# One source order for VectorE, ScalarE and GpSimd in attention, with decoding and the memory term cut into one phase per step

## The chip, the cores and the metric

The kernel runs on one core of one Trainium2 chip. The time is the device time of one execution in microseconds (us); the kernel before was timed three times, and the median of the three is its time. One further execution was profiled, and all rows below are from that one.

## What is computed

Inputs are fp32: q, k, v of shape (4, 8, 576, 64), a memory `M_prev` per head, and six weight matrices.

```python
scores = q @ k.T / 8, causal;  a = softmax(scores);  local = a @ v
q_p = phi(q)                                   # max(q, 0) + exp(min(q, 0))
mem = (q_p @ M_prev) / (q_p @ z_prev + 1e-6)
x = g * mem + (1 - g) * local                  # g = sigmoid(beta), per head
x = x.transpose(0, 2, 1, 3).reshape(2304, 512)
x = ((x @ w1) * (x @ w2)) @ w3 @ w_out         # 512 -> 1024 -> 1024 -> 512
h = x @ w_in                                   # 512 -> 2048
out = (h - tanh(h)) @ w_out2                   # 2048 -> 512
```

## The kernel before

**Weights.** The weights lie in memory as 64-bit patterns. A tile of 128 x 512 of them is loaded (`dec_load`, L64, tile `raw`) and decoded on the chip by `dec_ops`: GpSimd clamps the high words into T (L72) and makes E from them (L75), ScalarE rescales T (L77) and writes the low words into E (L79), VectorE merges the two (L82). The fp32 value is then split into two parts that are multiplied apart: GpSimd copies the high part (L94), VectorE subtracts it for the low part (L97). A `Decoder` runs this in four phases per tile. Where an fp32 product is wanted with such weights, three matmuls are issued: high x high, high x low, low x high.

**Folding.** `w3 @ w_out` is multiplied out beforehand, as 16 folds (f = 0..7 in two halves), during attention: 28 tiles are decoded there (8 of w_out, 16 of w3, 4 of w1 and w2), and `fold_pe` issues the matmuls in pieces: three matmuls a piece, four pieces a fold, 64 pieces in all (tile `fo`). After a fold ScalarE evacuates the first half (L268), or VectorE adds the second to it (L271) and the sum is split (L273, L274).

**Attention.** There are 16 pairs of heads P. Each has four steps, m = 4P + s: at s = 0 the row blocks u = 0 and 1 (128 rows each), at s = 1, 2, 3 the blocks u = 2, 3, 4 (the last has 64 rows). A step computes `scores` on TensorE (PSUM tile `sc`, 2 buffers), `rmax` (VectorE's reduction for the row maxima, L362), `exps` (ScalarE, L374, with the row sums), and `norm` (VectorE's reciprocal of the sums, L382 and L383, then GpSimd scales p by it, L388). Two steps later (`WAIT` = 2) `trans` transposes p on TensorE (PSUM tile `t`, 2 buffers), and `copy` moves it to SBUF as g0, g1 or g2: ScalarE four times in five (L399), VectorE else (L401). `av` multiplies g by v for the pair before: group 0 at s = 0, group 1 at s = 2; these are the matmuls `o<-g,v`, x20 for group 1. The pieces of the folds stand in the steps as `PIECES` says: 1, 2, 0 and 2 for the first eight pairs, 1, 1, 0 and 2 after. q and k of a pair are one tile `r` (3 buffers): SyncE issues its load (`load_qk`, L189) at s = 0, two pairs ahead, and ScalarE scales q by 1/8 (`scale_q`, L196) at s = 1 of the pair before its use.

**Memory term.** The first of six groups of 384 tokens is done within attention (`mem_early`), the other five later. For three tiles of 128 tokens (tile `mw`) `mem_a` runs on VectorE, ScalarE and GpSimd (products at L511 and L519), `mem_b` transposes (tile `mt`), and `mem_mm` does eight matmuls for each half of the heads (tile `mo`) and adds the result to x (L542). Tile `o` in PSUM has two buffers, which av, folds and `mo` share.

**What sets the order.** Only TensorE is held to the order of the source (`pinned`, L147). On VectorE, ScalarE, GpSimd and SyncE the scheduler picks by its own estimate of when an instruction can start. The background (decoding and the memory term) is given to it by `pump`, 2.2 times a step (`PACE`; 3.2 for the first `LEAD` = 10), each a phase, not before the step's maxima and exponentials (`issue_after`, `mark`). After attention (some 273 us) come the stages of the weight products, which the diff doesn't touch.

## Time and profile before

| what | us |
|---|---|
| three runs | 1012.65, 1011.66, 1015.96 |
| median | 1012.65 |
| profiled execution, its own time | 1016.29 |
| its span | 1014.5 |
| its mean granted clock (1 is full) | 0.988 |
| busy: TensorE | 959.7 (95%) |
| busy: weight loads | 818.1 (81%) |
| busy: VectorE | 660.1 (65%) |
| busy: ScalarE | 633.6 (62%) |
| busy: GpSimd | 409.1 (40%) |

The shares are means over all stages. The span runs from the first instruction to the last, and 1.8 us lie around it. PE is TensorE's matmuls, PEld its weight loads, DVE VectorE, ACT ScalarE, POOL GpSimd, SP SyncE. A number in square brackets behind an instruction is the time for which its engine stood idle before it, with what ended that time.

### The profile page before, as it was taken

Reading aid. Unit: us, or ns where it says so; the run is one execution under the profiler, and the core shown is the slowest. Engines: PE = TensorE matmul, PEld = TensorE weight load, DVE = VectorE, ACT = ScalarE, POOL = GpSimd, SP = SyncE. Lnnn points to the kernel's source line nnn. Section 1 sums busy time; section 2 is a strip of 40 time slices with the busy share of each in tenths; the row PEclk is TensorE's granted clock in tenths of the full one; section 3 lists DMA queues with packets and bytes.
Section 4 is the critical chain, followed back from the end, with each engine's and each line's share of the span. In section 5 each row is a group of like instructions: output and inputs, shape, how many; then the busy total and the mean of one; then the engine's idle time right before and its main releaser. Section 6 shows DMA issues by size and latency. Waiting matters only on the chain.

```text
span 1014.5 us, 16205 instructions
## 1 busy us (share of the span) xinstructions
PE 959.7 (95%) x5912; PEld 818.1 (81%) x5912; DVE 660.1 (65%) x1153; ACT 633.6 (62%) x1428; POOL 409.1 (40%) x500
## 2 busy tenths in 40 slices
PE   5899998969999899999999999999999999999998
PEld 2466555535698789999999999999999999998996
DVE  3655556766478765443212478888787787878875
ACT  5777767766655554244222668777776676767765
POOL 5757666765367552232000875222222222222222
PEclk9799999999999999999999999999999999999999
DMA  6443453433045562133000110000000000000000
GB/s 233 137 135 118 139 177 110 136 110 109 2 139 178 162 182 90 40 91 117 1 1 1 42 42 1 1 22 11 1 32 1 1 32 1 32 1 1 32 1 31
DMA packets 25807, 68.28 MB, mean 67 GB/s; under 512 B 4864, under 2 KB 5632, under 8 KB 25728
## 3 DMA queue, kind: packets, MB, share of 16 engines
q1 hardware_dynamic: 25728, 67.26, 20.8%
q8 instruction: 46, 0.75, 0.3%
q14 instruction: 33, 0.27, 0.1%
HBM read 62.53 MB, written 4.72 MB: 66 GB/s over the span
## 4 chain that ended last, share of the span: by engine, by line
PE 72%; DVE 8%; ACT 8%; DMA 6%; POOL 3%; issue 2%; SPq 0%; DVEq 0%; POOLq 0%; ACTq 0%
PE o L153 22%; PE h L153 20%; PE ab L153 15%; PE x L153 7%; DMA mw<-in_qt 3%; ACT p L374 3%; DMA r<-in_qk 2%; PE sc L153 2%; PE t L156 2%; PE fo L153 2%; DVE st L362 1%; ACT E L79 1%; POOL p L388 1%; ACT g L399 1%; ACT T L77 1%
## 5 line engine op out<-in xcount | busy, mean ns | idle before, releaser
L897 POOL TENSOR_TENSOR gl<-s,gh 128x384 fp32r<-128x384 f32 x96 | 99.6, 1038 | 287.9 <-ACT gh L891 273.0
L388 POOL TENSOR_SCALAR p<-p,st 128x128 f32<-128x128 f32 (+2 forms) x144 | 91.0, 645 | 59.5 <-ACT T L77 33.1
L153 PE MATMUL ab<-xh,wa 128*128 128x384 f32 x384 | 107.3, 340 | 4.3 <-DVE xs L542 3.2
L153 PE MATMUL x<-abh,wf 128*128 128x384 f32 x384 | 105.7, 340 | 2.2 <-ACT abh L696 2.2
L374 ACT ACTIVATE p<-sc,st 128x128 f32<-128x128 f32 (+2 forms) x144 | 78.0, 555 | 45.9 <-DVE st L362 39.3
L153 PE MATMUL ab<-xh,wb 128*128 128x384 f32 x384 | 105.7, 336 | 0.0
L873 DVE SCALAR_TENSOR_TENSOR s<-s,u 128x384 f32<-128x384 f32 x96 | 84.0, 875 | 25.0 <-ACT s L863 24.1
L869 ACT ACTIVATE u<-u,pc 128x384 f32<-128x384 f32 x96 | 59.4, 619 | 46.5 <-DVE s L873 46.5
L693 DVE TENSOR_TENSOR a<-ab,a 128x384 f32<-128x384 f32 x48 | 26.6, 553 | 83.2 <-PE ab L153 81.8
L153 PE MATMUL sc<-r 64*64 64x128 f32 (+4 forms) x640 | 72.2, 486 | 8.4 <-ACT r L196 5.9
L156 PE MATMUL t<-ident,p 128*128 128x128 f32 (+1 forms) x400 | 59.4, 285 | 21.6 <-ACT g L399 15.4
L75 POOL TENSOR_SCALAR E<-raw 128x512 f32<-128x512 f32 x72 | 59.5, 827 | 41.6 <-DVE z2p L82 7.6
L153 PEld LDWEIGHTS ab<-xh,wa 128*128 128x128 f32 x384 | 70.2, 188 | 7.2 <-DVE xs L542 4.8
L156 PEld LDWEIGHTS t<-ident,p 128*128 128x128 f32 (+1 forms) x400 | 46.2, 143 | 36.1 <-POOL p L388 16.8
L153 PEld LDWEIGHTS x<-abh,wf 128*128 128x128 f32 x384 | 70.1, 188 | 3.4 <-ACT abh L696 2.9
L861 ACT ACTIVATE u<-h 128x384 f32<-128x384 f32 x96 | 46.7, 487 | 41.5 <-PE h L153 41.5
L879 DVE TENSOR_TENSOR t<-h,t 128x384 f32<-128x384 f32 x96 | 53.1, 553 | 29.6 <-ACT t L862 29.2
L362 DVE TENSOR_REDUCE st<-sc 128x2 f32<-128x256 f32 (+4 forms) x80 | 62.5, 798 | 14.3 <-PE sc L153 13.4
L153 PEld LDWEIGHTS ab<-xh,wb 128*128 128x128 f32 x384 | 70.1, 188 | 0.3 <-ACT a L692 0.3
L878 DVE SCALAR_TENSOR_TENSOR s<-s,s 128x384 f32<-128x384 f32 x96 | 63.4, 661 | 8.7 <-DVE s L873 0.5
L72 POOL TENSOR_SCALAR T<-raw 128x512 f32<-128x512 f32 x72 | 52.3, 726 | 37.8 <-DMA raw<-in_wo 8.7
L79 ACT ACTIVATE E<-raw 128x512 uint16<-128x512 uint32 x72 | 56.8, 789 | 15.7 <-POOL E L75 14.9
(211 smaller groups left out, 2574.7 us busy)
## 6 DMA issues: line engine op xcount, KB each, us to landing
raw<-in_wo SPq DMA_DIRECT2D x24, 512.0 KB, 3.5
r<-in_qk SPq DMA_DIRECT2D x15, 576.0 KB, 4.6
raw<-in_w3t SPq DMA_DIRECT2D x16, 512.0 KB, 3.5
raw<-in_w SPq DMA_DIRECT2D x16, 512.0 KB, 3.5
raw<-in_wi SPq DMA_DIRECT2D x16, 512.0 KB, 3.5
v<-in_vt SPq DMA_DIRECT2D x16, 320.0 KB, 3.0
mw<-in_qt SPq DMA_DIRECT2D x18, 256.0 KB, 3.5
out<-ob SPq DMA_DIRECT2D x18, 256.0 KB, 2.3
```

The lines of the kernel that those rows point to most:

```text
L75: PO.tensor_scalar(out=e[:].bitcast(F32), in0=hw, scalar1=2.0 ** -100, scalar2=2.0 ** -53, op0=ALU.mult, op1=ALU.mult)
L79: AC.activation(out=e16, in_=lw, func=AF.Copy, scale=LOW_SCALE, bias=LOW_BIAS)
L153: return pinned(PE.matmul(o, lhsT, rhs, start=start, stop=stop))
L156: return pinned(PE.transpose(o, i, ident))
L362: mark["V"][m] = DV.tensor_reduce(out=st[:, 2 * x:2 * x + w], in_=seen(m, u, a), axis=AX.X if u < 4 else AX.XY, op=ALU.max, negate=True).ins
L374: mark["A"][m] = AC.activation(out=p[:, h], in_=sc[:, h], func=AF.Exp, bias=st[:, y:y + 1], accum_out=st[:, 4 + y:5 + y]).ins
L388: PO.tensor_scalar(out=pr, in0=pr, scalar1=sc, scalar2=1.0, op0=ALU.mult, op1=ALU.mult)
L869: AC.activation(out=u, in_=u, func=AF.Relu, bias=pc[:, 2:3])
L873: DV.scalar_tensor_tensor(out=s1, in0=s1, scalar=k2[0], in1=u, op0=ALU.add, op1=ALU.mult)
L878: DV.scalar_tensor_tensor(out=s1, in0=s2, scalar=k2[1], in1=s1, op0=ALU.add, op1=ALU.mult)
L879: DV.tensor_tensor(out=t, in0=o, in1=t, op=ALU.subtract)
L897: PO.tensor_tensor(out=l, in0=s1, in1=h[:].bitcast(F32), op=ALU.subtract)
```

## The change

A wrapper `Ordered` around TensorE, VectorE, ScalarE and GpSimd makes each instruction that is issued in attention depend, by order alone, on the one issued before it on its engine. SyncE isn't wrapped, and neither is anything that is issued after attention. `pump`, `PACE` and `issue_after` go. `background(m)` stands between `rmax` and `exps` of a step and advances every job by one phase: for a decoded tile GpSimd's two operations in one step, ScalarE's two and VectorE's merge in the next, the high copy and the low part in the third. The high copy moves from GpSimd to ScalarE. A tile is begun at every step for m < 8 and at every second after. The memory term goes by the same phases; at most one job with GpSimd work ("P") runs in a step. `fold_split` becomes a job of the next step, a decoded tile may be used one step later instead of two (`FLAG`), T has three buffers, E two, g1 one instead of two. `flush` (transposes and matmuls of the memory term) does at most one thing, at odd s or after the last scores.

```diff
-    PE, DV, AC, PO, SP = nc.tensor, nc.vector, nc.scalar, nc.gpsimd, nc.sync
+    SP = nc.sync
+    in_order, tail = [False], {}
+
+    class Ordered:
+        def __init__(self, engine):
+            self.engine = engine
+
+        def __getattr__(self, name):
+            call = getattr(self.engine, name)
+
+            def issue(*args, **kw):
+                i = call(*args, **kw)
+                if in_order[0]:
+                    if self.engine in tail:
+                        tc.add_manual_dep(i.ins, tail[self.engine].name, mybir.DependencyInfo(
+                            mybir.DependencyClass.NoSync, mybir.DependencyReason.DATA), reason="source order")
+                    tail[self.engine] = i.ins
+                return i
+
+            return issue
+
+    PE, DV, AC, PO = [Ordered(e) for e in (nc.tensor, nc.vector, nc.scalar, nc.gpsimd)]
...
-    in_order = [True]
-
-    def pinned(i):
-        if in_order[0]:
-            tc.keep_in_program_order(i)
-        return i.ins
...
-    ZB, FLAG, WAIT = 3, 2, 2
+    ZB, FLAG, WAIT = 3, 1, 2
     PIECES = ((1, 2, 0, 2), (1, 1, 0, 2))
-    PACE, LEAD = 2.2, 10
-    pace, WX = [0], (1, 3, 5, 7)
+    LEAD, WX = 8, (1, 3, 5, 7)
...
+    apt = att.enter_context(tc.tile_pool(name="apt", bufs=3))
...
+    def decode(k, raw, dst):
+        rb = raw[:].bitcast(U32).rearrange("p (n t) -> p n t", t=2)
+        lw, hw = rb[:, :, 0], rb[:, :, 1].bitcast(F32)
+        t = apt.tile([128, 512], U32, tag="T", name="T")
+        tf = t[:].bitcast(F32)
+        e = ap2.tile([128, 512], U32, tag="E", name="E")
+        PO.tensor_scalar(out=tf, in0=hw, scalar1=TOP, scalar2=-TOP, op0=ALU.min, op1=ALU.max)
+        PO.tensor_scalar(out=e[:].bitcast(F32), in0=hw, scalar1=2.0 ** -100, scalar2=2.0 ** -53,
+                         op0=ALU.mult, op1=ALU.mult)
+        yield "A"
+        e16 = e[:].bitcast(U16).rearrange("p (n t) -> p n t", t=2)[:, :, 0]
+        AC.activation(out=tf, in_=tf, func=AF.Copy, scale=REBIAS)
+        AC.activation(out=e16, in_=lw, func=AF.Copy, scale=LOW_SCALE, bias=LOW_BIAS)
+        DV.scalar_tensor_tensor(out=t, in0=t, scalar=3, in1=e, op0=ALU.logical_shift_left, op1=ALU.bitwise_or)
+        raws.popleft()
+        live[0] -= 1
+        ahead()
+        yield "A"
+        hi, lo = dst()
+        AC.activation(out=hi, in_=tf, func=AF.Copy)
+        DV.tensor_tensor(out=lo, in0=tf, in1=hi.bitcast(F32), op=ALU.subtract)
+        if k[0] in range(8):
+            folds.append((k, fstep[0]))
...
-                            WF[f] = wslot(wfp, f"wf{f}")
-                            AC.activation(out=WF[f][:, 0], in_=s, func=AF.Copy)
-                            DV.tensor_tensor(out=WF[f][:, 1], in0=s, in1=WF[f][:, 0].bitcast(F32), op=ALU.subtract)
+                            jobs.append(["A", fold_split(f, s)])
...
-                g_t[1] = ap2.tile([128, 4, 2, 320], F32, tag="g1", name="g1")
+                g_t[1] = ap1.tile([128, 4, 2, 320], F32, tag="g1", name="g1")
...
         def mem_early():
+            while folded[0] < 8:
+                yield "A"
             mem_setup()
             for g in range(EM):
                 while finished[0] < 8 * ((g * N + N - 1) // 576) + 8:
-                    yield 1
+                    yield "A"
                 mem_ms(g)
                 for tl in range(3):
                     while held[0] == 2:
-                        yield 1
+                        yield "A"
                     held[0] += 1
-                    qp = yield from mem_a(g, tl, (3 * g + tl) % 2)
-                    late.append((fstep[0] + 2, "t", tl, qp))
+                    a = mem_a(g, tl, (3 * g + tl) % 2, True)
+                    next(a)
+                    yield "A"
+                    yield "A"
+                    qp = yield from a
+                    late.append((fstep[0] + 1, "t", tl, qp))
                 for i in range(2):
-                    late.append((fstep[0] + 3 + i, "o", g, i))
+                    late.append((fstep[0] + 2, "o", g, i))
+                    yield "A"
 
         def flush():
-            while late and late[0][0] <= fstep[0] and not (late[0][1] == "o" and fold_open[0]):
-                _, k, x, y = late.popleft()
+            if late and late[0][0] <= fstep[0]:
+                _, k, x, y = late[0]
                 if k == "t":
                     mem_b(x, y)
                     held[0] -= 1
+                elif fold_open[0]:
+                    return None
                 else:
                     mem_mm(x, y)
+                late.popleft()
+                return k
...
+        def background(m):
+            pool = False
+            for j in list(jobs):
+                if j[0] == "P" and pool:
+                    continue
+                if j[0] == "P":
+                    pool = True
+                j[0] = next(j[1], None)
+                if j[0] is None:
+                    jobs.remove(j)
+            if pool or m < coming[0] or begun[0] == len(fold_seq):
+                return
+            k = fold_seq[begun[0]]
+            if k[0] in range(8) and coming[1:] and len(coming) - 1 - folded[0] >= ZB:
+                return
+            if k[0] in range(8):
+                coming.append(k)
+            begun[0] += 1
+            g = decode(*raws[live[0]])
+            live[0] += 1
+            jobs.append([next(g), g])
+            coming[0] = m + (1 if m < LEAD else 2)
...
-        for m in range(NM + 4):
+        in_order[0] = True
+        m = 0
+        while m < NM + 3 or jobs or late or folded[0] < 16 or begun[0] < len(fold_seq):
             P, s = divmod(m, 4)
             fstep[0] = m
             if m < NM:
                 scores(m)
                 rmax(m)
+            background(m)
+            if m < NM:
                 exps(m)
                 norm(m)
-            if s == 2 and P:
+            if s == 2 and 1 <= P <= 16:
                 av(P - 1, 1)
                 if P + 1 < 16:
                     load_v(P + 1)
-            if s == 0 and P:
+            if s == 0 and 1 <= P <= 16:
                 av(P - 1, 0)
-            for _ in range(PIECES[P >= 8][s]):
-                next(fold, None)
-            flush()
+            done = flush() if s % 2 or m >= NM else None
+            if done != "o":
+                for _ in range(PIECES[P >= 8][s]):
+                    next(fold, None)
             if 0 <= m - WAIT < NM:
                 for u in GROUPS[(m - WAIT) % 4]:
                     trans((m - WAIT) // 4, u)
-            if m < NM:
-                if s == 0 and 1 <= P <= 16 - RB:
-                    load_qk(P + RB - 1)
-                if s == 1 and P < 15:
-                    scale_q(P + 1)
-                with ExitStack() as e:
-                    for x in "VA":
-                        e.enter_context(tc.issue_after(mark[x][m]))
-                    pace[0] += PACE + (m < LEAD)
-                    while pace[0] >= 1:
-                        pump()
-                        pace[0] -= 1
-        while not wdec[0] or late or folded[0] < 16 or bg[1] is not False:
-            fstep[0] += 1
-            next(fold, None)
-            flush()
-            pump()
+            if done == "o":
+                for _ in range(PIECES[P >= 8][s]):
+                    next(fold, None)
+            if s == 0 and 1 <= P <= 16 - RB:
+                load_qk(P + RB - 1)
+            if s == 1 and P < 15:
+                scale_q(P + 1)
+            m += 1
         in_order[0] = False
+        wdec[0] = Decoder(w_items[NE:], 2, 3)
+        wdec[0].done, wdec[0].total = NE, 16
         pst.close()
         att.close()
```

How the order moves at three places follows; a row is one instruction, or one with its repeats, by the names of the program, and in the changed kernel all lines read L47 (the wrapper's).

ScalarE at the start of pair 5. First before: `r_1104` is q and k of pair 7, and the exponentials are the rows p, st.

```order
L399 ACTIVATE g1_1028<-t_1036 128x2x128
L196 ACTIVATE r_1104<-r_1104 128x576
L399 ACTIVATE xs1_422<-o_1081,omgt_85 128x4x64
L374 ACTIVATE p_1069,st_1066<-sc_1049,st_1066 128x128 x2
L374 ACTIVATE p_1072,st_1066<-sc_1049,st_1066 128x256 x2
L268 ACTIVATE wf3p_1090<-fo_939 128x512
L399 ACTIVATE g1_1028<-t_1092 128x4x128
L399 ACTIVATE g1_1028<-t_1098 128x4x128
L374 ACTIVATE p_1122,st_1120<-sc_1111,st_1120 128x384 x2
L77 ACTIVATE T_1109<-T_1109 128x512
L79 ACTIVATE E_1146<-raw_855 128x512
```

Now the change at the same place; `r_923` is q and k of pair 6.

```order
L47 ACTIVATE T_1026<-T_1026 128x512
L47 ACTIVATE E_1027<-raw_789 128x512
L47 ACTIVATE p_1081,st_1073<-sc_1056,st_1073 128x128 x2
L47 ACTIVATE p_1084,st_1073<-sc_1056,st_1073 128x256 x2
L47 ACTIVATE xs1_441<-o_1093,omgt_85 128x4x64
L47 ACTIVATE g1_1044<-t_1102 128x4x128
L47 ACTIVATE g1_1044<-t_1108 128x4x128
L47 ACTIVATE fo5_1127<-T_1026 128x512
L47 ACTIVATE p_1134,st_1125<-sc_1116,st_1125 128x384 x2
L47 ACTIVATE wf4p_1147<-fo_1040 128x512
L47 ACTIVATE g2_1045<-t_1155 64x128
L47 ACTIVATE r_923<-r_923 128x576
```

The scaling of pair 7's q stood ahead of pair 5's first exponentials; now that of pair 6 stands behind its second step, the decoding of a tile stands ahead of exponentials, and a high copy (`fo5`) is among them.

GpSimd in pair 13. First before; `mw` and `mst` are the memory term, and `mw_3271` and `mw_3348` belong to the five groups that come after attention in the source.

```order
L511 TENSOR_TENSOR mw_3271<-mw_3271,mc_1725 128x512
L72 TENSOR_SCALAR T_2770<-raw_2477 128x512
L388 TENSOR_SCALAR p_2584<-p_2584,st_2582 128x576
L519 TENSOR_TENSOR mw_3271<-mw_3271,mst_3278 128x512
L511 TENSOR_TENSOR mw_3348<-mw_3348,mc_1725 128x512
L519 TENSOR_TENSOR mw_3348<-mw_3348,mst_3429 128x512
L388 TENSOR_SCALAR p_2631<-p_2631,st_2628 128x128 x2
L388 TENSOR_SCALAR p_2634<-p_2634,st_2628 128x256 x2
```

And with the change:

```order
L47 TENSOR_TENSOR mw_3275<-mw_3275,mc_1648 128x512
L47 TENSOR_SCALAR p_2551<-p_2551,st_2542 128x512 x2
L47 TENSOR_TENSOR mw_3275<-mw_3275,mst_3282 128x512
L47 TENSOR_TENSOR mw_3352<-mw_3352,mc_1648 128x512
L47 TENSOR_SCALAR p_2594<-p_2594,st_2589 128x576
L47 TENSOR_SCALAR T_2645<-raw_2356 128x512
L47 TENSOR_SCALAR E_2646<-raw_2356 128x512
L47 TENSOR_TENSOR mw_3352<-mw_3352,mst_3433 128x512
L47 TENSOR_SCALAR T_3321<-raw_3192 128x512
L47 TENSOR_SCALAR E_3325<-raw_3192 128x512
L47 TENSOR_SCALAR p_2649<-p_2649,st_2636 128x128 x2
```

The later stage's instructions (`mw_3275`, `mw_3352`, and the decoding of `raw_3192`) aren't in the chain of order, and still stand among attention's.

TensorE, the memory term's matmuls `mo`. First before, in pair 13:

```order
L153 MATMUL fo_2589<-fo7_1432,zs_2275 128x512 x3
L153 MATMUL mo_2692<-mq0_1726,mc_1725 64x384 x2
L153 MATMUL mo_2693<-mq0_1726,mc_1725 64x384 x2
L153 MATMUL mo_2700<-mq1_1727,mc_1725 64x384 x2
L153 MATMUL mo_2701<-mq1_1727,mc_1725 64x384 x2
L156 MATMUL t_2708<-ident_82,p_2584 128x128 x4
L156 MATMUL t_2714<-ident_82,p_2584 64x128
L153 MATMUL sc_2724<-r_2270 64x512 x4
```

With the change, after the last scores:

```order
L47 MATMUL o_3137<-g0_3089,v1_108 64x256 x2
L47 MATMUL o_3137<-g0_3089,v1_108 64x128 x2
L47 MATMUL mo_3143<-mq0_1649,mc_1648 64x384 x2
L47 MATMUL mo_3144<-mq0_1649,mc_1648 64x384 x2
L47 MATMUL t_3151<-ident_82,p_3070 128x128 x4
L47 MATMUL t_3157<-ident_82,p_3070 128x128 x4
L47 MATMUL mo_3163<-mq1_1650,mc_1648 64x384 x2
L47 MATMUL mo_3164<-mq1_1650,mc_1648 64x384 x2
L47 MATMUL t_3171<-ident_82,p_3109 128x128 x4
L47 MATMUL t_3177<-ident_82,p_3109 64x128
```

They moved from the middle of pair 13 to behind the last scores; the rest of TensorE's order stays, but for the folds, which begin with two pieces at s = 3 of pair 1.

## Rows read from the trace of the kernel before

**Rows 1.** Busy time in five stretches: us, engines (x instructions), granted clock, DMA, GB/s

```profile
core 0: us, PE busy (x) PEld busy (x) DVE busy (x) ACT busy (x) POOL busy (x), PEclk, DMA share, GB/s
32.76:65.81 33.05, 29.35 (x249) 17.87 (x246) 20.52 (x42) 25.15 (x69) 22.11 (x34) 0.92 0.40 121
65.81:273.30 207.49, 185.57 (x1592) 114.29 (x1592) 131.96 (x280) 146.23 (x405) 128.04 (x183) 0.98 0.38 120
81.08:95.15 14.07, 14.07 (x126) 9.07 (x126) 8.59 (x19) 11.03 (x32) 9.14 (x14) 1.00 0.45 142
208.32:233.16 24.84, 18.85 (x143) 10.10 (x143) 15.94 (x36) 13.40 (x36) 14.76 (x20) 0.93 0.35 118
273.30:440.00 166.70, 156.35 (x953) 145.06 (x954) 107.65 (x195) 80.18 (x157) 81.01 (x92) 1.00 0.41 124
```

**Rows 2.** TensorE's timeline behind pair 4's mark and at attention's end: start us, busy us

```profile
87.64 0.45 PE L153 MATMUL sc<-r 64*64 64x128 f32 x8
...
89.35 0.95 PE L153 MATMUL fo<-z,zs 128*128 128x512 f32 x3
90.14 1.03 PE L156 MATMUL t<-ident,p 128*128 128x128 f32 x8
...
94.09 1.09 PE L153 MATMUL sc<-r 64*64 64x512 f32 x8
...
262.30 2.42 PE L153 MATMUL o<-g,v 128*64 128x320 f32 x20 [0.38 <-ACT g L399]
...
273.30 2.42 PE L153 MATMUL o<-g,v 128*64 128x320 f32 x20 [0.58 <-ACT g L399]
```

**Rows 3.** Waits, 0 to 280 us: us in total, times, longest us

```profile
ACT p L374 <- DVE st L362: 39.3, 27, 2.4
ACT r L196 <- DMA r<-in_qk: 18.9, 12, 3.2
...
PE t L156 <- ACT g L399: 15.4, 12, 2.6
```

**Rows 4.** ScalarE's timeline in pair 7

```profile
119.97 0.68 ACT L196 ACTIVATE r<-r 128x576 f32<-128x576 f32 x1 [2.54 <-DMA r<-in_qk]
...
120.91 0.36 ACT L374 ACTIVATE p<-sc,st 128x128 f32<-128x128 f32 x1
```

**Rows 5.** SyncE's timeline there

```profile
115.19 0.42 SPq L189 DMA_DIRECT2D r<-in_qk  x1
```

**Rows 6.** TensorE's timeline there

```profile
124.39 0.74 PE L156 MATMUL t<-ident,p 128*128 128x128 f32 x5 [1.47 <-ACT g L399]
```

**Rows 7.** GpSimd's timeline in pair 13

```profile
222.51 1.27 POOL L511 TENSOR_TENSOR mw<-mw,mc 128x512 f32<-128x512 f32 x1 [1.09 <-DMA mc<-in_zp]
225.72 1.04 POOL L519 TENSOR_TENSOR mw<-mw,mst 128x512 f32<-128x512 f32 x1 [1.94 <-DVE st L382]
226.75 1.62 POOL L388 TENSOR_SCALAR p<-p,st 128x128 f32<-128x128 f32 x4
```

**Rows 8.** TensorE's timeline in pair 13

```profile
227.37 1.33 PE L153 MATMUL mo<-mq,mc 64*64 64x384 f32 x8 [3.51 <-DVE s L271]
```

**Rows 9.** ScalarE and GpSimd by line and shape: xcount, busy us, mean ns, idle

```profile
L268 ACT ACTIVATE wf5p<-fo 128x512 f32<-128x512 f32 x1 | 0.6, 621 | 0.0
...
L94 POOL TENSOR_SCALAR zs<-T 128x512 fp32r<-128x512 f32 x16 | 9.9, 621 | 12.4 <-DVE T L82 12.4
```

**Rows 10.** GpSimd's, then ScalarE's and VectorE's timelines: operations of a loop of two steps

```profile
82.70 1.16 POOL L75 TENSOR_SCALAR E<-raw 128x512 f32<-128x512 f32 x1
83.93 0.67 POOL L72 TENSOR_SCALAR T<-raw 128x512 f32<-128x512 f32 x1
92.69 1.63 POOL L388 TENSOR_SCALAR p<-p,st 128x128 f32<-128x128 f32 x4 [0.44 <-DVE st L383]
...
122.50 0.65 ACT L77 ACTIVATE T<-T 128x512 f32<-128x512 f32 x1
123.02 0.79 ACT L79 ACTIVATE E<-raw 128x512 uint16<-128x512 uint32 x1
...
91.80 0.49 DVE L382 TENSOR_SCALAR st<-st 128x4 f32<-128x4 f32 x1 [0.81 <-ACT p L374]
92.32 0.18 DVE L383 RECIPROCAL st<-st 128x4 f32<-128x4 f32 x1
```

More of the change, by code (lines that the diff above doesn't have):

```diff
@@ L143, in run @@
             pass
-    in_order = [True]
-    def pinned(i):
-        if in_order[0]:
-            tc.keep_in_program_order(i)
-        return i.ins
     def mm(o, lhsT, rhs, start, stop):
-        return pinned(PE.matmul(o, lhsT, rhs, start=start, stop=stop))
+        return PE.matmul(o, lhsT, rhs, start=start, stop=stop).ins
     def tp(o, i):
-        return pinned(PE.transpose(o, i, ident))
+        return PE.transpose(o, i, ident)
     RB, HIP, SB, SN, NE, EM = 3, 1, 2, 2, 4, 1
@@ L232, in block_kernel @@
             fold_seq.append(("w", WX.index(f)))
-    fdec, folds, fstep, folded, fold_open = [None], deque(), [0], [0], [False]
-    def fold_dec():
-        d = fdec[0] = Decoder([fold_o_item(k[1]) if k[0] == "o" else w_items[k[1]] if k[0] == "w" else fold_item(*k)
-                                for k in fold_seq], 1, 3)
-        yield
-        while d.done < d.total:
-            k, n = fold_seq[d.done], d.done
-            d.step()
-            if d.done > n and k[0] in range(8):
-                folds.append((k, fstep[0]))
-            yield 1
+    folds, fstep, folded, fold_open = deque(), [0], [0], [False]
@@ new lines, in block_kernel, with ahead @@
+    jobs, todo, raws, live = [], deque(fold_seq), deque(), [0]
+    def ahead():
+        while todo and len(raws) < 3:
+            k = todo.popleft()
+            src, dst = fold_o_item(k[1]) if k[0] == "o" else w_items[k[1]] if k[0] == "w" else fold_item(*k)
+            raws.append((k, dec_load(src), dst))
+    def decode(k, raw, dst):
[21 more added lines that the diff above has]
+            folds.append((k, fstep[0]))
@@ L246, in fold_pe, with fold_split @@
+    def fold_split(f, s):
+        WF[f] = wslot(wfp, f"wf{f}")
+        AC.activation(out=WF[f][:, 0], in_=s, func=AF.Copy)
+        DV.tensor_tensor(out=WF[f][:, 1], in0=s, in1=WF[f][:, 0].bitcast(F32), op=ALU.subtract)
+        return
+        yield
     def fold_pe(psum):
@@ L496, in mem_m, with mem_a @@
             SP.dma_start(out=m.rearrange("p (a e) -> p a e", a=4), in_=mp[4 * b:4 * b + 4].rearrange("a p e -> p a e"))
-        def mem_a(g, tl, x):
+        def mem_a(g, tl, x, fine=False):
             t0 = g * N + tl * 128
@@ L507, in mem_a @@
             DV.tensor_scalar(out=e_, in0=qp, scalar1=0.0, scalar2=None, op0=ALU.min)
+            if fine:
+                yield "A"
             AC.activation(out=e_, in_=e_, func=AF.Exp)
-            yield 1
+            if not fine:
+                yield
             DV.scalar_tensor_tensor(out=qp, in0=qp, scalar=0.0, in1=e_, op0=ALU.max, op1=ALU.add)
+            if fine:
+                yield "P"
             PO.tensor_tensor(out=e_, in0=qp, in1=zb, op=ALU.mult)
-            yield 1
+            if not fine:
+                yield
             st = sm.tile([128, 24], F32, tag="mst", name="mst")
@@ L517, in mem_a @@
             DV.tensor_tensor(out=st[:, 0:8], in0=st[:, 16:24], in1=gates[:, 8:16], op=ALU.mult)
+            if fine:
+                yield "P"
             q3 = qp.rearrange("p (h d) -> p h d", h=8)
             PO.tensor_tensor(out=q3, in0=q3, in1=st[:, 0:8].unsqueeze(2).to_broadcast([128, 8, 64]), op=ALU.mult)
-            yield 1
+            if not fine:
+                yield
             return qp
@@ L588, in block_kernel @@
         fold = fold_pe(lambda: psA.tile([128, 512], F32, tag="o", name="fo"))
-        bg, pumps = [fold_dec(), None], [0]
-        next(bg[0])
-        def pump():
-            if bg[1] is None and folded[0] >= 8:
-                bg[1] = mem_early()
-            pumps[0] += 1
-            d = fdec[0]
-            k = fold_seq[d.done] if d.done < d.total else "-"
-            busy = k[0] in range(8) and len(fv) >= ZB and k not in fv or d.done == d.total
-            for x in (1, 0) if busy or pumps[0] % 3 == 0 else (0, 1):
-                if bg[x] and not (x == 0 and busy):
-                    if next(bg[x], None) is None:
-                        bg[x] = False
-                    else:
-                        return
-            if d.done == d.total and not wdec[0]:
-                wdec[0] = Decoder(w_items[NE:], 2, 3)
-                wdec[0].done, wdec[0].total = NE, 16
+        jobs.append(["A", mem_early()])
+        coming, begun = [0], [0]
+        ahead()
+        def background(m):
[12 more added lines that the diff above has]
+            if k[0] in range(8) and coming[1:] and len(coming) - 1 - folded[0] >= ZB:
+                return
+            if k[0] in range(8):
[5 more added lines that the diff above has]
+            coming[0] = m + (1 if m < LEAD else 2)
         load_qk(1)
```

3 lines of the change are left out of this document (1 added, 2 removed).

## The prediction

> **What bounds the kernel now.** I read first the windows, then TensorE's timeline, then the waits, then the timelines around the longest. The weight products from 273.30 us on keep TensorE at work (156.35 of the first 166.70 us) at full granted clock [rows 1], and the change doesn't touch them. So the question is attention, from 65.81 us (group 1 of av in pair 3) to 273.30 us (after the last pair): 207.49 us, of which PE works 185.57 at a mean granted clock of 0.98 [rows 1]. Pair 4, from 81.08 to 95.15 us, shows what a pair costs when nothing comes between: 14.07 us, all of it PE at granted clock 1.00. The pair from 208.32 to 233.16 us takes 24.84 [rows 1].
>
> What would PE need if every pair were like that? A piece of a fold takes 90.14 - 89.35 = 0.79 us [rows 2]. Pair 4 holds five, so a pair without them is 14.07 - 5 x 0.79 = 10.12. The last stretch (262.30 to 273.30, after 0.58 of waiting, four pieces) has no more scores: 11.00 - 0.58 - 3.16 = 7.26 [rows 2]. The memory term adds 12 transposes (1.03 / 8 each, 1.5) and 16 matmuls (1.33 / 8 each, 2.7), so 4.2 [rows 2, 8]. In the order of before, 56 pieces stand in this stretch: 12 x 10.12 + 7.26 + 56 x 0.79 + 4.2 = 177.1. So 207.49 - 177.1 = 30.4 us are lost, 21.92 of them as idle time and the rest as a lower clock.
>
> Where they are lost shows in three waits: ScalarE's exponentials wait 39.3 us for the row maxima, ScalarE's scaling of q waits 18.9 us in 12 places for the load of r, and PE's transposes wait 15.4 for ScalarE's copies [rows 3]. The second makes the third. SyncE issues r at 115.19 [rows 5]; ScalarE stands idle for 2.54 us until 119.97, when r has landed, with the next pair's exponentials queued behind until 120.91 [rows 4]; PE then waits 1.47 at 124.39 for a copy by ScalarE [rows 6]. r is not used until two pairs later; the scheduler put its scaling too early. In pair 13, GpSimd waits 1.09 for a DMA and 1.94 for VectorE, with the memory term, and the scaling of p (226.75) stands behind [rows 7]; PE waits 3.51 before its `mo` matmuls [rows 8].
>
> **The change part by part.**
>
> *q's scaling, by order.* It moves to s = 1 of the pair before its use, five steps after its load is issued. At 14.07 us for four steps that is 17.6 us, against 119.97 - 115.19 = 4.8 from issue to use now. SyncE isn't ordered, so the load may be issued later than now; 12.8 us are left for that. All 18.9 us of ScalarE's wait should go.
>
> *The high copies.* 28 copies go from GpSimd (0.621 us) to ScalarE, which takes 0.621 for a copy of the same size [rows 9]: 17.4 us more on ScalarE in attention. In pair 4 ScalarE works 11.03 us [rows 1]; with two copies it is 12.3 of 14.07. It fits beside PE, if what ScalarE does stands where it would wait for the maxima (39.3 us); that is where `background` stands. So I cost it at nothing; without that cover it would be the whole 17.4.
>
> Here a rule speaks against me. Pair 4 has ScalarE at 11.03 of 14.07 us (78%) and PE's weight loads at 9.07 (64%), while PE itself reads 100% [rows 1]. The Trainium skill, "Perfetto Trace Analysis", section "Identifying the Most-Contended Engine", says to judge ScalarE by its occupancy but TensorE by its weight loads, as matmuls are pipelined; by that ScalarE is the engine to relieve, and giving it work costs time. That is rival B below. I still take PE, since its rows there follow one on another with no wait shown.
>
> *The order of the four engines.* A wait can now hold up what stands behind it on the same engine. On VectorE, norm (which waits for the exponentials) stands ahead of the next maxima; on GpSimd, p's scaling ahead of the next decoding; on ScalarE, two decoding operations ahead of the exponentials. For what PE then still waits I take 0.3 us a pair, between the 0 of pair 4 and 1.3, what the others lose now (21.92 less the 24.84 - 18.85 of pair 13, by 12 [rows 1]): 13 x 0.3 = 3.9, bounds 0 and 17. The value lies near pair 4, whose order on PE is also that of the change.
>
> *Memory term.* It goes in fine phases, its `mo` matmuls move to the tail. But the later groups' instructions stay among attention's on GpSimd and aren't ordered. The pair took 24.84 us [rows 1], where a pair with four pieces (as from pair 8 on) and all of the 4.2 would take 10.12 + 3.16 + 4.2 = 17.5: 7.4 lost. I take 5, since PE no longer stands at `mo` there; the bounds are 2 and 11 (24.84 less a clean pair).
>
> *Tail.* Behind the last scores there is less to hide `mo` and the transposes, and g1 has one buffer: its next writer stands a step behind the av that reads it, so it should wait for nothing. 2.5, bounds 0 and 4.
>
> *The first three pairs.* One tile is begun at each step for m < 8, and ScalarE has its high copy too, but no wait for r. Two pieces (1.6 us) move there from the stretch above; it has 33.05 - 29.35 = 3.70 us of idle PE [rows 1]. I take 0, bounds -3 and 3.
>
> *Edits at nothing.* T's and E's buffers, `FLAG`, `fold_split` a step later: they move when work comes, and a fold has four pieces to wait with. The decoder for the 12 weights left is made after attention now; its loads can begin when raw buffers are free. 0, bounds -3 and 4.
>
> The sum from 65.81 to the mark at 273.30: 12 x 10.12 + 7.26 + 54 x 0.79 + 4.2 = 175.6 of PE work, and 3.9 + 5 + 2.5 of waits make 187.0, so 207.5 - 187.0 = 20.5 us are gained. Against the profiled execution, 1016.29 - 20.5 = 995.8; that execution lies 3.64 above the median of 1012.65, so the runs should give **992**. Its own bounds, with waits neither all low nor all high: 985 to 999.
>
> **The rivals.**
>
> *B: ScalarE becomes the bound, nothing is gained.* ScalarE loses 18.9 of waiting and takes 17.4 of copies; if each of its us counts, 1.5 are gained: 1011. For it speaks that ScalarE is the next busiest and that exponentials stand behind its decoding now; against it, that PE in pair 4 has no wait while ScalarE has 3 us to spare. 0.14.
>
> *C: slower, by a loop over two steps.* With source order a chain closes: exponentials, norm, p's scaling, the next tile's two operations on GpSimd, its two on ScalarE, and then exponentials again, since these now stand behind the decoding. At s = 0 it takes 1.59 (four exponentials, 120.91 to 122.50) [rows 4, 10], 0.67 for norm (0.49 + 0.18), 1.63 for p, 2.0 for GpSimd's two (82.70 to 84.70 by the rows: 1.16 + 0.67 and gaps), and 0.65 + 0.79 less overlap, 1.15, for ScalarE's [rows 10]: 7.0 us for two steps. PE needs 94.09 - 87.64 = 6.45 from the scores of s = 0 to those of s = 2 [rows 2], and the mean now is 207.49 / 13 / 2 = 8.0. So it is slower from 8.0 on. The other steps have shorter p, and only every second step has a tile; against it is also that the memory term comes in just a few pairs. If its products (1.27 and 1.04 [rows 7]) and unordered work of the later stage stretch the loop to 8.4, attention from pair 3 takes 13 x 16.8 = 218.4, 11 more: 1024. 0.14.
>
> *E: the order does not hold where it is needed.* SP and the later stage are outside of it. If the memory term loses 11 instead of 5, and loads that SP issues late cost each pair another 0.3 (4 in all), 10.5 of the gain are left: 1002. For it speaks GpSimd's order, where the later `mw` still stands ahead of p's scaling; against it, that this is one place in 16 pairs. 0.14.
>
> *D: nearly all of the lost time returns.* Waits of 1 us in all, and the first pairs lose their 3.70 of idle time: 207.49 - 175.6 - 1 + 3.7 = 34.6, so 978. For it speaks pair 4, which has no wait though ScalarE and GpSimd do the same work as in others; against it, that maxima, exponentials and copies of each step stay a chain between engines [rows 3]. 0.10.
>
> **How the numbers follow.** A measurement of this kernel can tell 0.5%, 5 us, from no change. The forecast has 0.48, D 0.10, E 0.14: faster, 0.72. B is the same, 0.14. C is slower, 0.14. The range reaches from D's 978 to B's 1011; C is left out, with the edges of B and D.
>
> **What would show it.** In the new profile ScalarE's wait for r is gone; pairs take 14.1 to 14.6 us; ScalarE works some 12.3 of them; no high copy stands on GpSimd in attention; the memory term's pair takes 15 to 19; and the mark at 273.30 comes at about 253. Wrong would be: exponentials that wait for E or T in each second step with pairs at 16 us or more (C), ScalarE without idle time at 15 to 16 (B), or GpSimd's p behind `mw` as now (E).

## The result, and the profile after

The changed kernel takes 1004.9 us (median of six, 1002.62 to 1008.11) against 1013.88 (median of six, 1011.66 to 1015.96). The ratio is 0.9914, 95% interval 0.989 to 0.9937. It is faster, as forecast, by 0.9%, but the gain is 9.0 us where 20.5 were forecast. 1004.9 lies outside the forecast's own bounds of 985 to 999; that it lies in the range of 978 to 1011 is luck, since only B's 1011 stretches the range that far. The profiled execution took 1003.38 (span 1001.6); it lies 1.5 below its median, and that of before 2.4 above its own, so the two profiles differ by 12.9.

The windows of the changed kernel answer to [rows 1]: the stretch of the first pairs, the one up to the mark after the last pair (group 1 of av, now at 258.81 us), pair 3, pair 12, and 166.70 us after attention.

```profile
30.53:59.28 28.75, 28.28 (x253) 18.12 (x253) 17.95 (x40) 25.29 (x70) 15.56 (x25) 1.00 0.40 137
59.28:258.81 199.53, 179.96 (x1594) 112.57 (x1586) 134.51 (x282) 161.14 (x428) 111.37 (x166) 0.99 0.40 124
59.28:73.34 14.06, 14.06 (x134) 9.05 (x126) 9.19 (x20) 12.95 (x35) 7.80 (x13) 1.00 0.43 142
197.64:216.85 19.21, 15.58 (x131) 9.01 (x124) 14.53 (x31) 13.39 (x36) 15.39 (x19) 0.91 0.39 129
258.81:425.51 166.70, 156.41 (x945) 145.07 (x946) 105.27 (x194) 79.17 (x155) 81.22 (x92) 0.99 0.40 124
```

The last mark comes 14.49 us earlier (273.30 before): 6.53 of it by the mark at 59.28 (65.81 before), 7.96 after it. Behind the mark 742.8 us follow, 741.2 before. In the long stretch PE's work fell by 5.6, by the granted clock (0.98 to 0.99) and two pieces that moved out (1.6), but its idle time only from 21.92 to 199.53 - 179.96 = 19.57. Yet the wait that I had held responsible is nearly gone, from 18.9 us in 12 places [rows 3] to 2.9 in two. ScalarE's waits up to 280 us:

```profile
ACT p L47 <- DVE st L47: 29.9, 41, 2.2
...
ACT r L47 <- DMA r<-in_qk: 2.9, 2, 1.8
```

So PE waits for something else. At the marks of pairs 5 to 9 it stands 0.44 to 1.54 us before av at s = 2, 4.9 in all; of the 19.57, 13.0 lie in pairs 8 to 12 (132.52 to 216.85 us, of which PE works 71.35). The timelines of ScalarE, VectorE and TensorE ahead of such a wait, in that order:

```profile
129.56 0.67 ACT L47 ACTIVATE zs<-T 128x512 fp32r<-128x512 f32 x1
130.08 0.62 ACT L47 ACTIVATE p<-sc,st 128x384 f32<-128x384 f32 x1
...
130.26 0.87 DVE L47 TENSOR_TENSOR zs<-T,zs 128x512 fp32r<-128x512 f32 x1 [0.35 <-ACT zs L47]
131.38 0.30 DVE L47 TENSOR_SCALAR st<-st 128x2 f32<-128x2 f32 x1 [0.26 <-ACT p L47]
131.71 0.17 DVE L47 RECIPROCAL st<-st 128x2 f32<-128x2 f32 x1
131.79 0.67 DVE L47 COPY g<-t 128x512 f32<-128x512 f32 x1
...
129.61 0.71 PE L47 MATMUL t<-ident,p 128*128 128x128 f32 x5
...
132.52 0.76 PE L47 MATMUL o<-g,v 128*64 128x320 f32 x4 [1.14 <-DVE g L47]
```

The transposes are done at 130.3, and VectorE could copy g then. But in source order two things stand ahead of the copy: a tile's low part, behind ScalarE's high copy, until 131.13, and `norm` of the same step, which waits for the exponentials, until 131.79. The copy comes 1.5 us later, 0.66 of it for norm, and av stands 1.14. Run 4 tells which of the two matters.

### The profile page after: what moved, and what is told of

The parts are those of the page before. It is cut to its first block, busy times and chain, and to the rows that moved or that the text cites. A ratio compares the mean times of both kernels' runs of the same rounds, so it can differ in the third digit from the quotient of the medians.

```text
span 1001.6 us, 16209 instructions
## 1 busy us (share of the span) xinstructions
PE 952.8 (95%) x5912; PEld 817.7 (82%) x5912; DVE 660.6 (66%) x1153; ACT 650.4 (65%) x1456; POOL 385.3 (38%) x472
## 4 chain that ended last, share of the span: by engine, by line
PE 74%; DVE 10%; ACT 7%; DMA 4%; POOL 3%; issue 2%; SPq 0%; DVEq 0%; ACTq 0%; POOLq 0%
PE o L47 23%; PE h L47 20%; PE ab L47 16%; PE x L47 8%; ACT p L47 4%; DMA mw<-in_qt 3%; DVE st L47 3%; PE sc L47 2%; PE t L47 2%; PE fo L47 2%; POOL mw L47 1%; DVE mst L47 1%; DVE mw L47 1%; POOL p L47 1%; ACT g L47 1%
## 5 line engine op out<-in xcount | busy, mean ns | idle before, releaser
L47 POOL TENSOR_TENSOR gl<-s,gh 128x384 fp32r<-128x384 f32 x96 | 99.9, 1041 | 287.7 <-ACT gh L47 272.8
L47 POOL TENSOR_SCALAR p<-p,st 128x128 f32<-128x128 f32 (+2 forms) x144 | 83.7, 595 | 94.4 <-DVE st L47 60.1
L47 PE MATMUL ab<-xh,wa 128*128 128x384 f32 x384 | 107.7, 341 | 4.4 <-DVE xs L47 3.4
L47 ACT ACTIVATE s<-u,pc 128x384 f32<-128x384 f32 x192 | 107.7, 614 | 0.6 <-POOL gl L47 0.6
L47 PE MATMUL x<-abh,wf 128*128 128x384 f32 x384 | 106.0, 340 | 2.2 <-ACT abh L47 2.2
L47 PE MATMUL ab<-xh,wb 128*128 128x384 f32 x384 | 105.6, 335 | 0.0
L47 DVE SCALAR_TENSOR_TENSOR s<-s,u 128x384 f32<-128x384 f32 x96 | 84.7, 883 | 25.7 <-ACT s L47 24.7
L47 ACT ACTIVATE p<-sc,st 128x128 f32<-128x128 f32 (+2 forms) x144 | 78.1, 553 | 30.1 <-DVE st L47 29.9
L47 ACT ACTIVATE u<-u,pc 128x384 f32<-128x384 f32 x96 | 59.4, 619 | 47.3 <-DVE s L47 47.3
L47 DVE TENSOR_TENSOR a<-ab,a 128x384 f32<-128x384 f32 x48 | 26.6, 554 | 82.8 <-PE ab L47 81.2
L47 PE MATMUL sc<-r 64*64 64x128 f32 (+4 forms) x640 | 69.0, 465 | 8.6 <-ACT r L47 5.8
L47 PEld LDWEIGHTS ab<-xh,wa 128*128 128x128 f32 x384 | 70.6, 189 | 7.3 <-DVE xs L47 5.0
L47 DVE TENSOR_REDUCE st<-sc 128x2 f32<-128x256 f32 (+4 forms) x80 | 62.9, 803 | 18.6 <-PE sc L47 17.8
L47 PEld LDWEIGHTS x<-abh,wf 128*128 128x128 f32 x384 | 70.4, 188 | 3.4 <-ACT abh L47 2.8
L47 ACT ACTIVATE u<-h 128x384 f32<-128x384 f32 x96 | 46.8, 488 | 40.2 <-PE h L47 40.2
L47 POOL TENSOR_SCALAR E<-raw 128x512 f32<-128x512 f32 x72 | 55.4, 769 | 43.2 <-DVE z2p L47 7.5
L47 DVE TENSOR_TENSOR t<-h,t 128x384 f32<-128x384 f32 x96 | 53.2, 554 | 28.4 <-ACT t L47 27.9
L47 PEld LDWEIGHTS ab<-xh,wb 128*128 128x128 f32 x384 | 70.1, 188 | 0.3 <-ACT a L47 0.3
L47 DVE SCALAR_TENSOR_TENSOR s<-s,s 128x384 f32<-128x384 f32 x96 | 63.5, 662 | 8.7 <-DVE s L47 0.5
L47 POOL TENSOR_SCALAR T<-raw 128x512 f32<-128x512 f32 x72 | 55.2, 767 | 33.4 <-DMA raw<-in_wo 8.8
L47 ACT ACTIVATE E<-raw 128x512 uint16<-128x512 uint32 x72 | 57.0, 792 | 15.0 <-POOL E L47 13.9
L47 PE MATMUL o<-g,v 128*64 128x320 f32 (+4 forms) x448 | 55.1, 379 | 12.1 <-ACT g L47 7.3
```

Source lines behind the costliest of these rows:

```text
L47: i = call(*args, **kw)
```

## The experiments

Each run's time is the median of its 5 to 12 executions, with the kernel before on the same chip at 1013.9 to 1014.5. "Mark" is the av of pair 3 in its profile, "stretch" the time from there to the last mark; behind that 739 to 744 us follow in every run but the tenth.

| run | median us | ratio, 95% | mark | stretch |
|---|---|---|---|---|
| before | 1013.88 | | 65.81 | 207.49 |
| the change | 1004.9 | 0.989 to 0.9937 | 59.28 | 199.53 |
| 1: before, q held | 1003.95 | 0.9877 to 0.9918 | 64.91 | 197.95 |
| 2: order on PE alone | 1013.29 | 0.997 to 0.9999 | 70.60 | 198.97 |
| 3: high copy on POOL | 1016.08 | 0.9996 to 1.0026 | 63.46 | 211.22 |
| 4: norm behind copies | 998.35 | 0.9818 to 0.986 | 61.48 | 195.68 |
| 5: later memory held | 1000.08 | 0.9845 to 0.9892 | 59.41 | 195.36 |
| 6: both (4 and 5) | 993.53 | 0.9782 to 0.9828 | 58.73 | 191.25 |
| 7: 6 without the memory term's first group | 981.02 | 0.9655 to 0.9698 | 59.05 | 178.81 |
| 8: 1 with the high copy on ACT | 1010.3 | 0.9948 to 0.9981 | 67.22 | 200.55 |
| 9: 6, norm late at s = 1 alone | 995.9 | 0.9799 to 0.984 | 59.27 | 191.23 |
| 10: 6, memory later | 1005.24 | 0.9884 to 0.9925 | 61.31 | 191.88 |
| 11: q behind its load | 1010.47 | 0.9942 to 0.9971 | 62.20 | 206.55 |

**1. The kernel before, with q's scaling held.**

```diff
                 if s == 1 and P < 15:
-                    scale_q(P + 1)
+                    with tc.issue_after(mark["A"][m]):
+                        scale_q(P + 1)
```

> The kernel before, with one thing changed: the scaling of the next pair's q may not stand ahead of the exponentials of its step (s = 1). ScalarE's 18.9 us of waiting for r should go. If these waits were what PE lost (my prediction's first term), attention ends some 10 to 19 us earlier: 995 to 1004. If they only stood where ScalarE and PE would have waited for something else, as the small gain of the change suggests, the time is within 4 us of before: 1010 to 1014, and PE's idle time in attention moves to other waits.

The time fell by 10.6 us, to that of the whole change (the intervals overlap), at the edge of the first outcome. ScalarE's wait for r is down to 3.2 us in two places, and three pairs in a row are clean, PE's av without a wait at 94.81, 108.97 and 123.20:

```profile
94.81 2.42 PE L153 MATMUL o<-g,v 128*64 128x320 f32 x20
108.97 2.42 PE L153 MATMUL o<-g,v 128*64 128x320 f32 x20
123.20 2.42 PE L153 MATMUL o<-g,v 128*64 128x320 f32 x20
```

The wait was a true cause, worth half of the 20.5 us of the forecast, and holding one instruction takes it away. "The second makes the third" held for about half: PE's wait for ScalarE's copies, 15.4 us before [rows 3], is 8.1 now.

```profile
PE t L156 <- ACT g L399: 8.1, 7, 2.1
```

If q's scaling is worth as much within the change, which no run shows, all else in the change nets to about nothing. The next runs look at what cancels.

**2. The change with the order on TensorE alone.**

```diff
-                if in_order[0]:
+                if in_order[0] and self.engine is nc.tensor:
```

> The changed kernel, its phases and background as they are, but the source's order held on TensorE alone; the scheduler orders the other three engines. If the source's order on the three is what gains, this goes back to 1010 to 1015. If the phases and the place of the background gain it, it stays at 1003 to 1007. If the order costs (copies of g behind norm and exponentials), it is faster than the changed kernel: 997 to 1002.

8.4 us slower than the change, the first of the outcomes. The stretch is the same (198.97); the first three pairs are what is lost, 11.3 us at the mark, which comes later even than before's (65.81). The edit also gives the place of q's scaling back to the scheduler, and part of ScalarE's wait for r returns, 5.0 of the 10.0 us ahead of the mark:

```profile
ACT r L47 <- DMA r<-in_qk: 10.0, 10, 2.2
```

How the 11.3 us divide between this wait and the rest of the order isn't shown.

**3. The high copies back on GpSimd.**

```diff
-        AC.activation(out=hi, in_=tf, func=AF.Copy)
+        PO.tensor_scalar(out=hi, in0=tf, scalar1=1.0, scalar2=1.0, op0=ALU.mult, op1=ALU.mult)
```

> The changed kernel with the 28 high copies back on GpSimd, in source order. Theory ScalarE: ScalarE works 12.5 to 13.8 us of pairs of 14.6 to 15.4 and bounds them; 17.4 us less of it give 8 to 15 us: 990 to 997, and pairs near 14.1. Theory chain: the pairs wait for the copy of g behind norm at s = 1, and ScalarE's copies matter only where they stand ahead of these exponentials: 1 to 5 us, 1000 to 1004. If GpSimd's p behind the high copy is late instead: 1005 to 1012.

11.2 us slower, the third of the outcomes and beyond it. GpSimd's, VectorE's and PE's timelines at s = 1 of one pair show a part of why:

```profile
104.26 1.28 POOL L47 TENSOR_SCALAR p<-p,st 128x128 f32<-128x128 f32 x3
105.51 0.62 POOL L47 TENSOR_SCALAR fo<-T 128x512 fp32r<-128x512 f32 x1
...
106.17 0.69 DVE L47 TENSOR_TENSOR fo<-T,fo 128x512 fp32r<-128x512 f32 x1 [1.32 <-POOL fo L47]
106.78 0.63 DVE L47 TENSOR_SCALAR st<-st 128x2 f32<-128x2 f32 x1
...
107.52 0.67 DVE L47 COPY g<-t 128x512 f32<-128x512 f32 x1
...
108.34 1.57 PE L47 MATMUL o<-g,v 128*64 128x320 f32 x10 [1.31 <-DVE g L47]
```

The copy stands behind p's scaling on GpSimd; VectorE's subtraction waits 1.32 for it, with norm and the copy of g behind, and PE stands 1.31 (1.17 to 1.88 at the marks of pairs 5 to 8, where the change has 0.44 to 1.20). But of the 11.7 us by which the stretch is longer, pairs 3 to 7 hold only 2.3. Pairs 8 to 12, in which the memory term runs, hold 9.4 (the change first, then this run):

```profile
132.52:216.85 84.33, 71.35 (x627) 44.07 (x628) 60.45 (x134) 66.76 (x177) 52.70 (x73) 0.98 0.43 136
```

```profile
139.02:232.75 93.73, 75.54 (x627) 46.54 (x628) 60.23 (x134) 62.21 (x167) 56.15 (x81) 0.93 0.38 122
```

At the one place there that I show, a product of the memory term stands ahead of the high copy as well; VectorE waits 2.60 and PE 3.56:

```profile
153.15 1.04 POOL L47 TENSOR_TENSOR mw<-mw,mst 128x512 f32<-128x512 f32 x1
...
154.81 0.69 DVE L47 TENSOR_TENSOR zs<-T,zs 128x512 fp32r<-128x512 f32 x1 [2.60 <-POOL zs L47]
...
156.43 4.52 PE L47 MATMUL o<-g,v 128*64 128x320 f32 x20 [3.56 <-DVE g L47]
```

The forecast of theory ScalarE failed: with 17.4 us less to do there, the kernel is slower. What relief of ScalarE is worth without the new wait on GpSimd, this run can't tell; run 4 says more.

**4. norm behind the step's copies.**

```diff
                 exps(m)
-                norm(m)
...
             if 0 <= m - WAIT < NM:
                 for u in GROUPS[(m - WAIT) % 4]:
                     trans((m - WAIT) // 4, u)
+            if m < NM:
+                norm(m)
```

> The changed kernel with norm (VectorE's sum and reciprocal, GpSimd's p) issued behind the step's transposes and copies, so that VectorE's copy of g no longer waits for the exponentials of the same step. Theory chain: PE's 4.3 us of waits for VectorE's g at av go, gain 2 to 4 us: 1001 to 1003. Theory ScalarE: nothing, within 2 us of 1005. Where p comes too late for its transposes two steps later, slower: up to 1012.

6.5 us faster than the change, more than expected. VectorE still makes the low part first, but copies g before norm, and PE's av follows its scores with no wait (VectorE, then PE):

```profile
101.94 0.87 DVE L47 TENSOR_TENSOR fo<-T,fo 128x512 fp32r<-128x512 f32 x1 [0.37 <-ACT fo L47]
102.72 0.68 DVE L47 COPY g<-t 128x512 f32<-128x512 f32 x1
103.33 0.15 DVE L47 TENSOR_SCALAR st<-st 128x2 f32<-128x2 f32 x1
...
103.52 0.22 PE L47 MATMUL sc<-maskb,identb 64*64 64x128 bf16 x4
103.67 1.03 PE L47 MATMUL o<-g,v 128*64 128x320 f32 x6
```

So it was norm that made the copy late. Three pairs in a row take 42.19 us, PE at work in all of them, with ScalarE, high copies included, busy for 38.37; in these pairs ScalarE doesn't hold PE up:

```profile
61.48:103.67 42.19, 42.19 (x386) 27.16 (x378) 28.53 (x58) 38.37 (x105) 24.30 (x40) 1.00 0.44 141
```

**5. The later memory groups held.** Instructions of the memory term's later groups get the order dependency on attention's last instruction of their engine.

```diff
-                if in_order[0]:
+                if in_order[0] or behind[0]:
...
-                    tail[self.engine] = i.ins
+                    if in_order[0]:
+                        tail[self.engine] = i.ins
...
-                if next(mem[0], mem) is not mem:
+                behind[0] = True
+                r = next(mem[0], mem)
+                behind[0] = False
+                if r is not mem:
```

> The changed kernel; the memory term's later groups may not start on VectorE, ScalarE and GpSimd ahead of attention's last instruction there. Theory later stage (my rival E): their two tiles stand in pairs 12 and 13 between decoding and maxima and cost these pairs some 3 to 5 us; without them the time is 999 to 1002. Rival: they only fill time, and doing them after attention costs as much, or delays the first of the later groups: 1004 to 1008.

4.8 us faster than the change, as theory later stage had it. Pairs 11 to 13, the change first and this run second:

```profile
180.95:232.28 51.33, 43.20 (x373) 26.34 (x373) 37.40 (x81) 40.89 (x108) 34.81 (x47) 0.97 0.43 135
```

```profile
179.38:228.25 48.87, 42.77 (x374) 26.39 (x374) 33.37 (x71) 40.16 (x107) 27.79 (x43) 0.97 0.40 131
```

VectorE has ten instructions less there and GpSimd four, and 2.5 us are gained; 1.7 more are gained in pair 10 (17.72 to 16.03 us).

**6. Both.**

> Both edits together: norm behind the copies of its step, and the later groups of the memory term held behind attention. If their costs lie in different pairs they add: 998.4 less what the hold alone gains on the changed kernel, 994 to 997. If one wait takes the place of the other: 998 to 1002.

993.53, just under the first outcome: the two gains add, and this is the fastest of the whole kernels, 0.9782 to 0.9828 of before.

**7. No memory term in attention.**

```diff
-        jobs.append(["A", mem_early()])
...
+        mem_setup()
+        mem_ms(0)
```

> As the run before, but the memory term's first group of 384 tokens is left out altogether (the later five groups are done). PE's own work for it is 4.2 us. If its phases on VectorE, ScalarE and GpSimd are what stretches pairs 9 to 12 (15.8 to 18.6 us instead of about 14), the time falls by 12 to 18 against the run before, to 980 to 986. If pairs 9 to 12 are slow for the four tiles of w1 and w2 or for having four pieces instead of five, it falls by 4 to 7.

This kernel leaves out the memory term of the first 384 tokens, so it computes less than the others. 12.5 us less, the first of the outcomes. The stretches of run 6 and of this one:

```profile
58.73:249.98 191.25, 177.68 (x1594) 111.89 (x1586) 130.62 (x271) 159.03 (x426) 106.83 (x163) 1.00 0.39 127
```

```profile
59.05:237.86 178.81, 173.14 (x1565) 110.18 (x1558) 124.05 (x248) 153.74 (x418) 98.61 (x157) 1.00 0.39 127
```

Of 12.44 us, 4.54 are PE's own work and 7.90 idle time (13.57 against 5.67). So the term costs PE nearly twice as much in waits as in work of its own.

**8. Run 1 with the high copies on ScalarE.**

```diff
-                                for k in fold_seq], 1, 3)
+                                for k in fold_seq], 1, 3, hip=0)
```

> The kernel before with the scaling of q held (first run of this study, 1003.95) and, besides, the 28 high copies in attention on ScalarE. If GpSimd's late p is what costs there too (the change lost 11 us when they went back to GpSimd), a gain of 3 to 8: 996 to 1001. If it is only under the source's order that GpSimd stands in the way, since there p queues behind the copy, no gain, 1003 to 1006; if ScalarE is full, up to 1010.

6.4 us slower than run 1. The same move that gains 11 us in source order loses under the scheduler's. The pairs between 80 and 145 us that are clean in run 1 (14.04 to 14.23 us) take 15.1 to 15.6 here. ScalarE isn't full in these four pairs, busy for 49.52 of 61.46 us. In the first of them PE is at work throughout, at a granted clock of 0.90; in the other three it stands 3.3 us, 1.31 of them for GpSimd's scaling of p. Which ScalarE instruction is behind this I haven't shown.

**9. norm late at s = 1 alone.**

```diff
-                norm(m)
+                if s != 1:
+                    norm(m)
...
+            if m < NM and s == 1:
+                norm(m)
```

> As the run with both edits (norm late, later memory held; 993.53), but norm stands behind the copies only at s = 1, where av is next. If the wait at av for the copy of g at s = 1 is what the edit removes, the gain stays whole: 991 to 995. If the copies at other steps matter as much, half of it is lost: 996 to 998.

995.9, 2.4 us above run 6 and between the two outcomes; the intervals overlap. The stretch is 191.23 against 191.25, so in the profiles the s = 1 step, whose copies av needs next, is where the order mattered from pair 3 on. In the first pairs 0.5 us are lost again (mark at 59.27 against 58.73).

**10. The memory term later.**

```diff
-            while folded[0] < 8:
+            while folded[0] < 8 or begun[0] < 26:
```

> As the run with both edits (993.53), but the memory term's first group begins only when 26 of the 28 tiles are begun, so that its phases run in pairs 13 to 15 and not in 9 to 12. If its cost (12.5 us, of which 4.2 are PE's own) comes from sharing VectorE and ScalarE with the decoding, most of the other 8.3 goes: 985 to 989. If it comes from the phases standing in the chain of each step (they are ahead of the exponentials wherever they run), or is paid in a longer tail: 991 to 997.

Worse than both outcomes, by 11.7 us against run 6. GpSimd, VectorE and PE at the memory term's first tile:

```profile
196.99 1.03 POOL L47 TENSOR_SCALAR T<-raw 128x512 f32<-128x512 f32 x1
198.11 1.01 POOL L47 TENSOR_SCALAR E<-raw 128x512 f32<-128x512 f32 x1
199.19 0.65 POOL L47 TENSOR_SCALAR T<-raw 128x512 f32<-128x512 f32 x1
199.92 0.69 POOL L47 TENSOR_SCALAR E<-raw 128x512 f32<-128x512 f32 x1
200.71 1.64 POOL L47 TENSOR_SCALAR p<-p,st 128x128 f32<-128x128 f32 x4
202.31 1.27 POOL L47 TENSOR_TENSOR mw<-mw,mc 128x512 f32<-128x512 f32 x1
...
203.61 0.69 DVE L47 TENSOR_REDUCE mst<-mw 128x8 f32<-128x512 f32 x1 [3.37 <-POOL mw L47]
...
206.19 0.68 DVE L47 COPY g<-t 128x512 f32<-128x512 f32 x1
206.93 4.52 PE L47 MATMUL o<-g,v 128*64 128x320 f32 x20 [5.21 <-DVE g L47]
```

Two tiles are decoded in a row on GpSimd. The source begins at most one a step in attention, so the other is of the stage after attention, which isn't ordered. The memory term's product comes behind them and p, VectorE stands 3.37 for it with a copy of g behind, and PE stands 5.21. Even so the stretch is that of run 6 (191.88), since pairs 8 to 11 take 13.8 to 14.3 us. Against run 6 the profile loses 10.9 us in the tail, 751.7 us behind the last mark, and 2.6 in the first pairs; what makes the tail longer I haven't shown.

**11. q's scaling behind its load.**

```diff
                 load_qk(P + RB - 1)
-            if s == 1 and P < 15:
-                scale_q(P + 1)
+                scale_q(P + RB - 1)
+            if P == 0 and s in (1, 2):
+                scale_q(s)
```

> The changed kernel with one part undone: q of the pair after next is scaled at s = 0 right behind the issue of its load, as the scheduler had it before. ScalarE then waits for the DMA (4.6 us from issue to landing) with the exponentials or copies of that step behind it, in 13 pairs. If the place of this one instruction is what the change gained by, all of the gain goes and more: 1014 to 1035. If other edits of the change hide the wait (decoding ahead of it), 1005 to 1010.

5.6 us slower, at the upper edge of the second outcome, and it missed what it was for. In source order the scaling stands behind the copies of s = 0, and by then r has mostly landed; ScalarE's waits for r and the place:

```profile
ACT r L47 <- DMA r<-in_qk: 3.2, 2, 2.1
```

```profile
103.66 0.72 ACT L47 ACTIVATE r<-r 128x576 f32<-128x576 f32 x1
104.24 0.67 ACT L47 ACTIVATE fo<-T 128x512 fp32r<-128x512 f32 x1
104.76 0.62 ACT L47 ACTIVATE p<-sc,st 128x384 f32<-128x384 f32 x1
```

It shows another thing: a scaling of 0.72 us ahead of the high copy and the exponentials of s = 1 costs about what it takes. Pairs 4 to 7 take 15.3 to 15.5 us, 15.40 in the mean, where the change's take 14.80. How much q's old place would cost within the change stays open.

## Why the prediction was wrong, and where it was right

The sign and the wait for r came out, the size did not. The steps that failed are two terms of the sum: PE's remaining waits, taken at 0.3 us a pair, and the memory term, taken at 5 us.

*The sign and q's scaling.* Right in mechanism: the wait went, and run 1 shows that taking it away in the kernel before was worth 10.6 us by itself. The sum has no price for it alone; it let 20.5 of the 30.4 lost us return, because PE's waits named ScalarE behind it. With it gone, the next chain ends last.

*"For what PE then still waits I take 0.3 us a pair."* This is the step that failed first. The sum held 187.0 us for the stretch, the change took 199.53, 12.5 more: 8.2 of them idle time of PE (19.57 where the sum had 11.4), and 4.4 PE at work for longer (179.96 where it had 175.6), in part for the granted clock of 0.99 (run 7, at 1.00, has 173.14 where the sum without the memory term has 171.4). In the profiles the place of norm alone is worth 3.9 (the change against run 4) and 4.1 (run 5 against run 6). It lies in a chain that I hadn't listed: scores, maxima, exponentials, norm, copy of g, av. I had named norm's wait for the exponentials, but looked at the maxima behind it, not at the copy. Taking pair 4 of before as the model was wrong, since only PE's order was the same there.

*"I take 5" for the memory term.* Too low. The term costs 12.4 in its own right (runs 6 and 7) where the sum had 4.2 + 5 = 9.2, and the later groups' instructions, which I had as rival E, 4.2 more in the stretch (the change against run 5). It isn't one pair's matter either, as I had it: 9.0 of the 12.4 lie in pairs 8 to 12 (79.79 us in run 6, 70.78 in run 7). Without the memory term's 9.2 my sum is 187.0 - 9.2 = 177.8, and run 7 took 178.81: the PE floor and the small waits came out together within 1.0 us once both orders were mended. Counted from there, the 12.5 are 1.0, then 3.2 for the memory term, 4.1 for norm's place and 4.2 for the later groups. Each of these is a difference of two single profiles; by the medians norm's place is worth 6.5 and the later groups 4.8.

*The high copies at nothing.* It holds under the source order: pair 3 takes 14.06 us with PE at work throughout and ScalarE at 12.95. The Trainium skill, "Perfetto Trace Analysis", "Identifying the Most-Contended Engine", has the engine with the highest occupancy optimized first, with TensorE judged by its weight loads; here that is ScalarE, and rival B. Run 4 speaks against it here: in three pairs PE works all of 42.19 us while ScalarE is busy for 38.37. But I had missed that the move is itself worth 11.2 us within this order (run 3), since it takes a wait for GpSimd out of VectorE's way. And run 8 shows that the same copies do cost where the scheduler places them.

*The first three pairs, 0 within 3.* Out of its bounds: 6.5 us gained at the mark. Run 1 has only 0.9 there, so it isn't q alone, and run 2 loses 4.8, so it is the source's order on the three engines that gains them; q's place is a part of that order. A part is the granted clock, 0.92 before [rows 1] and 1.00 now.

*After attention, 0 within -3 and 4.* Right, 1.6 lost.

*The rivals.* C, the loop over two steps, didn't close: a pair with a tile at every second step runs at 14.06 us. D let PE wait for 1 us in all; it stands 19.57. E's 1002 came nearest, and the half of it on the later stage held (run 5); the half on late loads didn't, as ScalarE waits for r in two places only, 2.9 us.

## What to carry to other kernels

Find the one instruction that waits for a DMA with urgent work queued behind it before ordering everything: holding that one instruction gave as much as this whole change. When engines keep the source's order, place each instruction by who needs its result soonest, and ask of every instruction that waits what stands behind it; here a copy behind `norm` cost 6.5 us by the medians, some 4 in the stretch of the profiles. A price for moved work holds only for the order that it was read in: the same copies, moved to ScalarE, gained 11 us in one order and cost 6 in another. And an order that ends with a stage doesn't keep the next stage's instructions out of it.
